# Dealing 1.5 MB of zeros to the DMA engines in other shares and from other SBUF rows, in a decode kernel that writes a gradient

## The chip, the cores and the metric

One core of one Trainium2 chip runs the whole program in one launch. The metric is the device time of that launch in microseconds, the median of several runs. One run was also recorded by the hardware profiler; its trace has every instruction, and every packet that the core's 16 DMA engines moved, with start, length, bytes and queue. A packet's record does not say which of the 16 engines moved it.

## The reference

A decode step of attention beside a gated feed-forward block, and the gradient of both. Four batch rows (`B = 4`), one token each, model width 512, 32 query heads on 8 key/value heads of width 128, a cache of 4096 positions of which only the last 1024 take part:

```python
k = jnp.repeat(k_cache[:, :, Sk - W:, :], rep, axis=1)     # W = 1024, Sk = 4096
v = jnp.repeat(v_cache[:, :, Sk - W:, :], rep, axis=1)
scores = jnp.einsum("bhqd,bhkd->bhqk", q, k) * (Dh ** -0.5)
p = _softmax(scores, axis=-1)
o = jnp.einsum("bhqk,bhkd->bhqd", p, v)
...
return x + _A_ref(xn, ...) + _B_ref(xn, ...)
...
_out, _vjp = jax.vjp(_f, A_x, A_k_cache, A_v_cache, A_wq, A_wo, B_w_gate, B_w_up, B_w_down)
_grads = _vjp(grad_out)
```

The gradients of the two caches have the shape of the whole caches. For the 3072 positions ahead of the window they are zero, and these zeros have to be written: 2 caches x 4 batches x 8 heads x 3072 x 128 numbers of 2 bytes, 50.3 MB. All of the data moved, weights, windows, gradients and zeros, is 111.9 MB.

## The kernel before

Five engines work side by side: TensorE multiplies, VectorE and ScalarE transpose, mask and empty the accumulators, GpSimd (POOL in the profile) clears tiles and copies small blocks, and SyncE (SP) issues nearly all transfers, in an order written out by hand. A transfer that SP issues goes through SP's own queue, a transfer that GpSimd issues through GpSimd's queue, and both are carried out by the same 16 DMA engines.

The stages in order: the weights of the feed-forward block and of the attention are loaded (lines 161 to 166 and 325 to 328); the feed-forward block and its gradients (up to line 451); the key and value windows, two buffers each, and per batch the scores, the softmax, and the gradients of keys and values (the loop at line 675); the last phase from line 769 on, in which the gradients of `wo` and `wq` are made in eight pieces of 1 MB and stored through `result` (line 116).

**The zeros.** `ztile` (line 223) holds zeros, 128 partitions of 12,288 bytes. The zeros to be written are cut into 32 groups of two heads (`ztodo`, line 281), 1.5 MB each. Such a group is 64 rows by 2 heads, 128 pieces of 12,288 bytes: row `m` is positions `48 m` to `48 m + 47`, and a piece is one row of one head. `zeros(n)` (line 298) lets SP write the next `n` groups: 64 rows are read from every second partition of `ztile`, each row for two pieces. `result` calls it ahead of each store by the counts in `before` (line 114); the loads of keys and values are followed by it too (lines 461 to 463, 731, 752). `zeros` makes a group wait for the group four earlier (`deep`).

31 of the 32 groups go that way. The last of the list, `zog, zb, zg` (line 283), is GpSimd's: `part_zeros(m0, rows, each, part, after)` (line 285) writes `rows * each` rows of it from `m0` on. Its source is `rows` partitions of `ztile`, starting at partition `part` and four apart, and each of them serves `2 * each` pieces. Before the change there are four calls: three on lines 422 to 424, right after GpSimd cleared its tiles of the feed-forward stage, while the weights are still loading (15 + 2 + 15 rows, from 3, 2 and 3 partitions), and one on line 819, at the start of the last phase (32 rows from 8 partitions), which waits for the group of SP last issued there (`zdone[-1]`).

So in the code before, the number of pieces for one source partition is 10, 2 and 10 in the three early calls, and 8 in the late one.

**Waits of SP.** Besides data and buffers, a transfer of SP waits until the completion semaphore that it is given is free. There are eight of them, given out in turn, so a transfer waits for the one eight before it.

Of the kernel before, what the change touches and what calls it, by code (L numbers as in the profile page):

```python
# [19 lines left out]
def kernel(  # L20
# [24 lines left out]
    nc = tc.nc  # L45
# [7 lines left out]
    K0 = Sk - W  # L53
# [29 lines left out]
    def evac(out, in_, n):  # L83

        ca, cd = (190 + n) / 1.2, (130 + n) / 0.96
        eng = "act" if load["act"] + ca <= load["dve"] + cd else "dve"
        load[eng] += ca if eng == "act" else cd
        if eng == "act":
            return nc.scalar.copy(out=out, in_=in_)  # L89
        return nc.vector.tensor_copy(out=out, in_=in_)  # L90

    def t32(out, in_, n):
        load["dve"] += (130 + n) / 0.96
        nc.vector.transpose(out=out, in_=in_)  # L94

    def pairs(ap):
        return ap.bitcast(U32)

    def scratch():
        return scrp.tile([P, 1024], U32, name="scr", tag="scr")  # L100
# [6 lines left out]
    def stg_tile():  # L107

        if not halves:
            pair = stg_pair()  # L110
            halves.extend(pair[:, h] for h in range(2))
        return halves.pop(0)
# [3 lines left out]
    def result(*parts):  # L116
        zeros(min(before.popleft(), len(ztodo)))
        for out, in_ in parts:
            nc.sync.dma_start(out=out, in_=in_)
# [19 lines left out]
    def mm(out, lhsT, rhs, first=True, last=True, pos=None):  # L139
        kw = {} if pos is None else {"tile_position": pos}  # L140
        nc.tensor.matmul(out, lhsT=lhsT, rhs=rhs, start=first, stop=last, **kw)  # L141

    def bank(name, tag="w", shape=(P, 512), dt=FP32):
        pool = {"w": ps_w, "x": ps_x}.get(tag, ps_a)
        return pool.tile(list(shape), dt, name=name, tag=tag)
# [75 lines left out]
    ZP = P // 2  # L221
    ZW = K0 // ZP * Dh
    ztile = const.tile([P, ZW], BF16, name="ztile")
# [36 lines left out]
    def window(dram, b, h):  # L260

        return dram[b, h * G // 2:(h + 1) * G // 2, K0:Sk, :].rearrange("g (m j) d -> m g (j d)", j=2 * J)

    def alternate(tl, h):

        t_ = tl[h:h + 1]
        return bass.AP(tensor=t_.tensor, offset=t_.offset,
                       ap=[[2 * t_.ap[0][0], P // 2], [2 * J * Dh, G // 2], [1, 2 * J * Dh]])

    def load_kv(b, k, pool, tag, eng, **kw):  # L270
        d_, src = ((k_t, A_k_cache), (v_t, A_v_cache))[k]
        tl = pool.tile([P, G // 2, 2 * J, Dh], BF16, name=tag, tag=tag)
        for h in range(2):
            with tc.high_priority():
                d = eng.dma_start(out=alternate(tl, h), in_=window(src, b, h), **kw)
        d_[b] = tl
        return d

    ZG = 2
    zsrc = bass.AP(tensor=ztile.tensor, offset=ztile.offset, ap=[[2 * ztile[:].ap[0][0], ZP], [0, ZG], [1, ZW]])  # L280
    ztodo = [(og, b, g) for b in range(B) for g in range(0, G, ZG) for og in (out_2, out_3)]
    zdone = []
    zog, zb, zg = ztodo.pop()

    def part_zeros(m0, rows, each, part, after=None):

        z = nc.gpsimd.dma_start(  # L287
            out=zog[zb, zg:zg + ZG, 0:K0, :].rearrange("g (m j) d -> m g (j d)", m=ZP)[m0:m0 + rows * each],
            in_=bass.AP(tensor=ztile.tensor, offset=ztile[part:part + 1, :].offset,
                        ap=[[4 * ztile[:].ap[0][0], rows], [0, ZG * each], [1, ZW]]))  # L290
        if after is not None:
            behind(z.ins, after.ins)

    def behind(ins, other):
        tc.add_manual_dep(ins, other.name,
                          mybir.DependencyInfo(mybir.DependencyClass.Sync, mybir.DependencyReason.DATA))

    def zeros(n, after=None, deep=4):

        for _ in range(n):  # L300
            og, b, g = ztodo.pop(0)
            z = nc.sync.dma_start(out=og[b, g:g + ZG, 0:K0, :].rearrange("g (m j) d -> m g (j d)", m=ZP), in_=zsrc)
            if len(zdone) >= deep:
                behind(z.ins, zdone[-deep].ins)
            if after is not None:
                behind(z.ins, after.ins)
            zdone.append(z)


    if True:  # L310
# [5 lines left out]
        def flat(t_):  # L316
            return t_[:].rearrange("p f c -> p (f c)")
# [92 lines left out]
        for wi, (wsb, dh, og) in enumerate(((wu_sb, dhu, out_7), (wg_sb, dhg, out_6))):  # L410
            dh_f = flat(dh)
            dhr = hgu[:].rearrange("p u f c -> p (u f c)").bitcast(BF16)
            for a, q in enumerate(quad):
                ps = bank("rep_ps", "w", (P, FQ))
                mm(ps[:], rsum_b[q, :], dh_f[q, :], pos=(Q * a, 0))
                evac(dhr[:, a * FQ:(a + 1) * FQ], ps[:], FQ)
            dhP = scratch()[:, 0:FPB * Q].rearrange("p (f x) -> p f x", f=FPB)
            t32(dhP, pairs(dhr[:, 0:F]), 896)
            dhs = ffn.tile([P, FPB, 2, 4 * B], BF16, name="dhs", tag=f"dhs{wi}")
            nc.gpsimd.memset(dhs[:], 0.0)  # L420
            if wi == 1:
                part_zeros(0, 3, 5, 0)
                part_zeros(15, 2, 1, 12)
                part_zeros(17, 3, 5, 20)
            dhPb = dhP.bitcast(BF16).rearrange("p f (x r) -> p f r x", r=2)
            for a, q in enumerate(quad):
                nc.vector.tensor_copy(out=dhs[q, :, :, a * B:(a + 1) * B], in_=dhPb[q, :, :, 0:B])
            for ch in range(4):
                sc = scratch()
                n7 = FPB // 4  # L430
                t32(sc[:, 0:n7 * P].rearrange("p (k c n) -> p c k n", k=n7, c=C),
                    pairs(wsb[:])[:, :, ch * n7 * Q:(ch + 1) * n7 * Q], 896)
                sb = sc[:, 0:n7 * P].bitcast(BF16).rearrange("p (k n r) -> p k r n", k=n7, r=2)
                for k in range(n7):
                    c = nm % 4
                    mm(dxf_ps[quad[c]].rearrange("p r n -> p (r n)"), dhs[:, ch * n7 + k].rearrange("p r x -> p (r x)"),
                       sb[:, k], nm < 4, nm >= 2 * FPB - 4, (0, Q * c))
                    nm += 1
            dwg_v = og.rearrange("(p h c) f -> h p (c f)", h=2, c=2)
            for h in range(2):  # L440
                stg = stg_tile()
                for ci in range(2):
                    for a, q in enumerate(quad):
                        ps = bank("dwg_ps", "w", (P, FQ))
                        mm(ps[:], xn_b[q, 2 * h + ci:D:C], dh_f[q, :], pos=(Q * a, 0))
                        o_ = (ci * NQ + a) * FQ
                        evac(stg[:, o_:o_ + FQ], ps[:], FQ)
                result((dwg_v[h], stg[:, 0:2 * F]))
# [4 lines left out]
    with tc.tile_pool(name="mid", bufs=1, reuse_waits="tile") as mid:  # L453
# [4 lines left out]
        with (tc.tile_pool(name="kvp", bufs=1, reuse_waits="tile") as kvp,  # L458
              tc.tile_pool(name="att", bufs=1, reuse_waits="tile") as att):
            load_kv(0, 1, kvp, "va", nc.sync)  # L460
            zeros(2)
            load_kv(1, 0, kvp, "kb", nc.sync)
            zeros(4)


# [2 lines left out]
            rows = [qm[:], dyBD[:].rearrange("p n r x -> p (n r x)").rearrange("p (b g d) -> p b g d", b=B, g=4)]  # L468
# [132 lines left out]
            def small(name, shape=(P, 1)):  # L601
                return att.tile(list(shape), FP32, name=name, tag=name)
# [72 lines left out]
            for b in range(B):  # L675
                S = sps[0][:]
                m = small("m")
# [124 lines left out]
            for i in range(KH):  # L802
                t, e, c = i // 8, i // 4 % 2, i % 4
# [12 lines left out]
            s_o = sums[:, 0:D]  # L816
            TT(out=s_o, in0=ob_ps[:], in1=fo[:], op=ALU.add)

            part_zeros(32, 8, 4, 64, zdone[-1])
            dwo_v = out_5.rearrange("(p t k) n -> t p (k n)", t=4, k=8)  # L820
            dwq_v = out_4.rearrange("(p c) j -> c p j", c=C)
            late = {}
# [126 lines left out]
```

## Time and profile before

| | |
|---|---|
| median of 3 runs | 272.11 us (272.02 to 273.19) |
| the profiled execution | 272.15 us |
| its span in the trace | 270.4 us |
| data moved | 111.90 MB, mean 414 GB/s; 30.68 MB read from and 81.01 MB written to HBM |
| busy share: PE, DVE, ACT, POOL | 61%, 67%, 51%, 13% |
| packets | 16,640 |

The span is the profiled execution between its first and last instruction; the 1.75 us between it and the 272.15 us lie around it. Times in the trace count from the start of the span. "SPq" and "POOLq" are an engine's issuing of transfers, not the transfer itself. A transfer of 1.5 MB of zeros takes SP about a microsecond to issue and lands about 19 us later.

### The profile page before, as it was taken

What the parts mean: (1) busy time and instruction counts of PE and PEld (TensorE: products, weight loads), DVE (VectorE), ACT (ScalarE), POOL (GpSimd) and SP (SyncE); (2) the same over time, 40 slices, a digit from 0 to 9 for tenths busy, and PEclk for the clock granted to TensorE, in tenths of its full rate; (3) what the DMA queues carried; (4) which work ended last, traced back from release to release, by engine and by line L of the source; (5) the groups of instructions that cost most, each with busy time, mean ns of one, the idle gap of its engine ahead of it and who ended that gap; (6) DMA issues with size and microseconds to landing.
All of it is one profiled execution on the core that took longest, in us unless ns stands there. A gap on an engine that the chain in (4) does not pass through costs nothing.

```text
span 270.4 us, 3304 instructions
## 1 busy us (share of the span) xinstructions
PE 164.6 (61%) x1152; PEld 62.0 (23%) x1159; DVE 180.5 (67%) x339; ACT 137.4 (51%) x278; POOL 36.1 (13%) x95
## 2 busy tenths in 40 slices
PE   1256988968536687676568578585877898460000
PEld 0121342222112342123222233122421223010000
DVE  7869768978798428873588536793289999970000
ACT  2242775670022636696577765696476666460000
POOL 8900002091032101120012100000000000000000
PEclk9998885556855555997999975997577999555555
DMA  7999999999999999999999999999999999999994
GB/s 264 437 422 449 409 369 425 430 431 413 421 426 428 430 412 425 426 421 427 415 421 418 433 416 421 431 422 431 418 428 425 422 429 417 429 429 428 428 420 207
DMA packets 16640, 111.90 MB, mean 414 GB/s; under 512 B 1760, under 2 KB 1776, under 8 KB 10992
## 3 DMA queue, kind: packets, MB, share of 16 engines
q1 hardware_dynamic: 16072, 110.12, 97.7%
q0 software_dynamic: 544, 1.57, 1.5%
q8 instruction: 9, 0.15, 0.2%
q14 instruction: 7, 0.06, 0.1%
q10 hardware_dynamic: 8, 0.00, 0.0%
HBM read 30.68 MB, written 81.01 MB: 413 GB/s over the span
## 4 chain that ended last, share of the span: by engine, by line
DVE 21%; PE 21%; ACT 17%; issue 4%; ACTq 0%
DVE scr L94 9%; ACT stg L124 6%; ACT spr L584 5%; PE kv_ps L141 4%; PE dw_ps L141 4%; DVE stg L124 3%; PE sc_ps L141 3%; PE ok_ps L141 2%; DVE odt L647 2%; PE od_ps L141 2%; ACT late L124 2%; DVE dqs L763 2%; DVE wq_t L94 2%; PE ob_ps L141 1%; ACT last L124 1%
## 5 line engine op out<-in xcount | busy, mean ns | idle before, releaser
L124 ACT CAST stg<-kv_ps 128x512 bf16<-128x512 f32 x102 | 54.6, 598 | 26.5 <-PE kv_ps L141 26.4
L141 PE MATMUL sc_ps<-scr,bd 128*32 128x256 bf16 x256 | 20.1, 399 | 18.1 <-DVE scr L94 17.5
L141 PEld LDWEIGHTS <-spr 128*128 128x128 bf16 x256 | 17.0, 108 | 36.1 <-issue 24.3
L141 PE MATMUL kv_ps<-dyBD,spr 128*128 128x512 bf16 x60 | 24.1, 528 | 1.9 <-issue 1.3
L141 PE MATMUL kv_ps<-qm,spr 128*128 128x512 bf16 x63 | 19.7, 387 | 3.0 <-DVE stg L124 1.1
L94 DVE STREAM_TRANSPOSE scr<-va 128x1024 uint32<-128x1024 uint32 x16 | 19.5, 1224 | 0.0
L124 DVE CAST stg<-kv_ps 128x512 bf16<-128x512 f32 x10 | 6.6, 688 | 17.9 <-PE kv_ps L141 17.9
L89 ACT CAST stg<-dwg_ps 128x448 bf16<-128x448 f32 x26 | 12.0, 567 | 3.3 <-DMA out_dram<-stg 2.4
L549 POOL COPY bd<-D3q 32x64 bf16<-32x64 bf16 x32 | 7.6, 245 | 44.4 <-PE sc_ps L141 43.2
L141 PEld LDWEIGHTS <-bd 128*32 128x32 bf16 x256 | 6.3, 99 | 29.8 <-issue 27.2
L141 PE MATMUL dw_ps<-scr,xn_b 32*128 32x512 bf16 x32 | 9.4, 545 | 5.5 <-ACT late L124 4.0
L124 ACT CAST late<-dw_ps 128x512 bf16<-128x512 f32 x16 | 9.2, 588 | 6.8 <-PE dw_ps L141 6.7
L141 PE MATMUL do_ps<-scr,dyBD 128*128 128x512 bf16 x31 | 11.1, 491 | 2.3 <-DVE scr L94 1.9
L584 ACT ACTIVATE spr<-dS_b,amask 64x256 bf16<-64x256 bf16 x16 | 7.4, 554 | 8.5 <-DVE dS_b L728 8.5
L549 POOL COPY bd<-D3d 32x64 bf16<-32x64 bf16 x32 | 7.4, 239 | 31.7 <-PE sc_ps L141 16.4
L647 DVE SCALAR_TENSOR_TENSOR odt<-od_ps,om,odt 128x128 f32<-128x128 f32 x12 | 4.2, 351 | 11.1 <-ACT odt L642 10.8
L124 DVE CAST stg<-dw_ps 128x512 bf16<-128x512 f32 x16 | 10.5, 685 | 1.5 <-PE dw_ps L141 1.3
L287 POOL DMA_DIRECT2D out_dram<-ztile x4 | 3.0, 753 | 61.9 <-DMA out_dram<-ztile 61.9
L94 DVE STREAM_TRANSPOSE scr<-wo_sb 128x1024 uint32<-128x1024 uint32 x8 | 9.8, 1237 | 1.6 <-PE do_ps L141 1.0
L124 ACT CAST stg<-dw_ps 128x512 bf16<-128x512 f32 x16 | 8.9, 588 | 3.6 <-PE dw_ps L141 3.4
L94 DVE STREAM_TRANSPOSE scr<-ka 128x1024 uint32<-128x1024 uint32 x8 | 9.8, 1233 | 1.2 <-PE r_ps L141 1.1
L124 DVE CAST late<-dw_ps 128x512 bf16<-128x512 f32 x16 | 10.4, 675 | 0.3 <-PE dw_ps L141 0.3
(203 smaller groups left out, 337.4 us busy)
## 6 DMA issues: line engine op xcount, KB each, us to landing
out_dram<-ztile SPq DMA_DIRECT2D x31, 1536.0 KB, 19.1
out_dram<-stg SPq DMA_DIRECT2D x18, 1024.0 KB, 14.7
va<-in_A_v_cache_dram SPq DMA_DIRECT2D x8, 1024.0 KB, 14.3
out_dram<-stg SPq DMA_DIRECT2D x6, 896.0 KB, 11.9
wq_sb<-in_A_wq_dram SPq DMA_DIRECT2D x1, 4096.0 KB, 27.9
wo_sb<-in_A_wo_dram SPq DMA_DIRECT2D x1, 4096.0 KB, 37.3
ka<-in_A_k_cache_dram SPq DMA_DIRECT2D x4, 1024.0 KB, 15.6
kb<-in_A_k_cache_dram SPq DMA_DIRECT2D x4, 1024.0 KB, 19.0
```

Of the source, the lines that this page charges most:

```text
L89: return nc.scalar.copy(out=out, in_=in_)
L94: nc.vector.transpose(out=out, in_=in_)
L124: return nc.scalar.copy(out=out, in_=in_) if eng == "act" else nc.vector.tensor_copy(out=out, in_=in_)
L141: nc.tensor.matmul(out, lhsT=lhsT, rhs=rhs, start=first, stop=last, **kw)
L287: z = nc.gpsimd.dma_start(out=zog[zb, zg:zg + ZG, 0:K0, :].rearrange("g (m j) d -> m g (j d)", m=ZP)[m0:m0 + rows * each], in_=bass.AP(ten ...
L549: nc.gpsimd.tensor_copy(out=t_[q, :, :, g2, :, o_:o_ + 4], in_=src[q, b, g2])
L584: nc.scalar.activation(out=out, in_=in_, func=ACT.Copy, scale=amask[q, a:a + 1])
L647: STT(out=t_[:], in0=ps[:, g, :], scalar=(om, oms)[k][:, g:g + 1], in1=t_[:], op0=ALU.mult, op1=ALU.add)
L763: nc.vector.tensor_copy(out=dqs[q, :, :, :, a * B + b], in_=d3v[q])
```

## The change

The address of GpSimd's group is set up once as `zpart`. `part_zeros` reads partitions eight apart instead of four apart. The early calls become two: 5 rows from 5 partitions (0, 8, 16, 24, 32; 2 pieces each) and 32 rows from 8 partitions (40, 48, ... 96; 8 pieces each). The late call becomes two of 12 rows from 3 partitions each (104, 112, 120, then 0, 8, 16; 8 pieces each). The 3 rows that are left, 17 to 19, 6 pieces or 73,728 bytes, are written by SP in a new transfer, `rest_zeros(17, 20)`, between its load of `kb` and the four groups of zeros behind it. That transfer cuts the three rows of each of the two heads into 8 packets of 4608 bytes; its destination has the shape 2 x 8 x 2304, its source is 16 partitions.

```diff
+    zpart = zog[zb, zg:zg + ZG, 0:K0, :].rearrange("g (m j) d -> g m (j d)", m=ZP)
+
     def part_zeros(m0, rows, each, part, after=None):
 
         z = nc.gpsimd.dma_start(
-            out=zog[zb, zg:zg + ZG, 0:K0, :].rearrange("g (m j) d -> m g (j d)", m=ZP)[m0:m0 + rows * each],
+            out=zpart[:, m0:m0 + rows * each].rearrange("g m e -> m g e"),
             in_=bass.AP(tensor=ztile.tensor, offset=ztile[part:part + 1, :].offset,
-                        ap=[[4 * ztile[:].ap[0][0], rows], [0, ZG * each], [1, ZW]]))
+                        ap=[[8 * ztile[:].ap[0][0], rows], [0, ZG * each], [1, ZW]]))
         if after is not None:
             behind(z.ins, after.ins)
+
+    def rest_zeros(m0, m1):
+
+        n = (m1 - m0) * ZW // 8
+        nc.sync.dma_start(out=zpart[:, m0:m1].rearrange("g m e -> g (m e)").rearrange("g (k e) -> g k e", k=8),
+                          in_=bass.AP(tensor=ztile.tensor, offset=ztile.offset, ap=[[8 * ztile[:].ap[0][0], 16], [1, n]]))
...
             if wi == 1:
-                part_zeros(0, 3, 5, 0)
-                part_zeros(15, 2, 1, 12)
-                part_zeros(17, 3, 5, 20)
+                part_zeros(12, 5, 1, 0)
+                part_zeros(20, 8, 4, 40)
...
             load_kv(1, 0, kvp, "kb", nc.sync)
+            rest_zeros(17, 20)
             zeros(4)
...
-            part_zeros(32, 8, 4, 64, zdone[-1])
+            part_zeros(52, 3, 4, 104, zdone[-1])
+            part_zeros(0, 3, 4, 0, zdone[-1])
```

The instructions of TensorE, VectorE and ScalarE are the same, in the same order. GpSimd issues four transfers as before, two early and two late instead of three and one. SP issues one transfer more.

## The prediction

> **What bounds the kernel now.** First the page's slices, then its queues, then the busy time by stretches, then the issues at the end.
>
> ```profile
> DMA  7999999999999999999999999999999999999994
> GB/s 264 437 422 449 409 369 425 430 431 413 421 426 428 430 412 425 426 421 427 415 421 418 433 416 421 431 422 431 418 428 425 422 429 417 429 429 428 428 420 207
> ...
> q1 hardware_dynamic: 16072, 110.12, 97.7%
> q0 software_dynamic: 544, 1.57, 1.5%
> q8 instruction: 9, 0.15, 0.2%
> q14 instruction: 7, 0.06, 0.1%
> ```
>
> The 16 DMA engines are full from the first slice to the last. q1 is SP's queue, q0 GpSimd's; q8 and q14 fetch the program itself.
>
> ```profile
> 180.00:240.00 60.00, 45.10 (x303) 15.05 (x303) 47.29 (x87) 38.60 (x77) 0.65 (x1) 0.77 1.01 425
> 240.00:265.00 25.00, 1.83 (x7) 0.33 (x5) 2.58 (x4) 2.35 (x4) 0.00 (x0) 0.50 1.01 427
> 265.00:270.40 5.40, 0.00 (x0) 0.00 (x0) 0.00 (x0) 0.00 (x0) 0.00 (x0) 0.50 0.36 152
> ```
>
> Columns: the stretch, its length, busy time of PE, PEld, DVE, ACT, POOL, granted clock, DMA share, GB/s. From 243 us on no engine computes, and the DMA engines still work at 427 GB/s up to 265 us; then the share falls to 0.36.
>
> ```profile
> 241.20 0.61 SPq L302 DMA_DIRECT2D out_dram<-ztile  x1
> 243.78 4.03 SPq L119 DMA_DIRECT2D out_dram<-late  x2
> 249.90 3.99 SPq L119 DMA_DIRECT2D out_dram<-stg  x2
> ```
>
> SP issues its last store before 253.9 us, and the data of it lands until 268.9 us: 15 us of work are queued when nothing is left to compute. So bytes bound the kernel, and neither GpSimd's time nor an earlier landing of weights can move the end. The bytes are the same after the change. What is left is how evenly the 16 engines end.
>
> **How the engines end.** The packet records name no engine. But a packet starts 3 ns ahead of the end of the one before it on its engine, and each engine has the same known order of SP's packet sizes; strung together by these two rules, the records from 33 us on fall into 16 chains without a gap. Their last packets end at (us of the span):
>
> ```
> GpSimd's pieces     chains, end of the last packet
> call of 32 rows, 8  268.88  266.90 266.65 266.61 266.59 266.56 266.55 266.48
> 2nd call of 15, 10  267.72  267.57  266.51
> 1st call of 15, 10  267.56  267.33  267.22
> call of 2 rows,  2  268.93  265.11
> mean of the 16      267.20
> ```
>
> The pieces of the last call lie on eight chains, those of the third call on three others. The small transfers of 4 rows have 4 packets of 1 KB, and these lie on four chains, 267.56, 267.33, 267.22 and 265.11. Of the five chains without a third or fourth call, 265.11 must be one with 2 pieces, as it ends 2 us ahead of its three mates. So GpSimd's queue deals engines in turn, 0 to 2, 3 and 4, 5 to 7, 8 to 15, and small transfers go to 0 to 3; engine 3 ends at 265.11 and engine 4 at 268.93.
>
> Two chains end 1.2 us behind all others. Engine 4 has just 2 pieces, but its packets of 12,288 bytes take 476 ns in the mean, those of the other 15 chains 460 to 462: 248 of them make 4 us. The other, at 268.88, is one of the eight with 8 pieces. It carries two of q8's nine fetches (0.94 us each), its mates one or none, and its 4 KB packets take 161.0 ns against some 159.7 (512 of them, 0.7 us). After 268.93 the program needs 1.4 us to close (270.36), and 1.75 us lie around the span: 272.15 us, against the median of 272.11.
>
> **The change part by part.** A piece of 12,288 bytes takes 460 ns and moves its chain on by 457.
>
> ```profile
> out_dram<-ztile POOLq DMA_DIRECT2D x1, 768.0 KB, 11.9
> out_dram<-ztile POOLq DMA_DIRECT2D x2, 360.0 KB, 25.1
> out_dram<-ztile POOLq DMA_DIRECT2D x1, 48.0 KB, 21.9
> ```
>
> Columns: how many issues, the size of one, us until it landed.
>
> GpSimd's calls of 5, 8, 3 and 3 partitions are dealt in the same way: engines 0 to 4 (2 pieces each), 5 to 12 (8), 13 to 15 (8), 0 to 2 (8). Together: 0 to 2 have 10 as before, 3 and 4 have 2 as before, 8 to 15 have 8 as before, 5 to 7 have 8 instead of 10. The six pieces that these three lose (0.91 us each) are those which SP writes. So engine 4 stays at 268.93, the other late chain at 268.88, engine 3 at 265.11, and 5 to 7 come to 266.8, 266.7 and 265.6, where it gains nothing.
>
> SP's new transfer: 16 packets of 4608 bytes. The trace has none of this size. The nearest are 4096 bytes (median 159 ns) and 7168 (272 ns); between them, nearer the first, I take 175. How many engines share it isn't shown either. The 4-row transfers run on 4 engines, and every transfer with 64 or 128 rows on 16, so the outermost count seems to decide; here it is 2 on the side of HBM and 16 on the side of SBUF. I take 2, the count that both sides can be cut into by their outermost rows, on the engines that the small transfers use first: engines 0 and 1 get 8 packets, 8 x 0.175 = 1.40 us. They come from among 267.22, 267.33 and 267.56, and so end at 268.6 to 268.96. Bounds of the price: 8 x 0.159 = 1.27 and 8 x 0.272 = 2.18 us, so 268.5 to 269.7. If all 16 share it, each gets one packet: 0.16 to 0.27 us on all, and engine 4 ends at 269.1.
>
> [...]
>
> Other source partitions: GpSimd's pieces took 460 ns from partitions four apart, as SP's did from its own rows, so I put the move at nothing. Bounds: one piece of the 128 took 794 ns; one to three such on the engine that ends last would be 0.3 to 1 us; below nothing it can't go, as 460 is what every undisturbed packet of this size takes.
>
> Early and late: 74 pieces instead of 64 ahead of the weights, at most 8 on an engine instead of 10, so the weights land up to 0.9 us sooner; 48 instead of 64 later. This moves work in time on engines that are never idle, and costs nothing as long as each has something queued. The cover is the 15 us at the end; at 67 us, where SP's new transfer is put, four groups of 1.5 MB follow, and a group lands 19 us after its issue. GpSimd issues two transfers (0.75 us each) at each place; nothing of weight is queued behind them.
>
> The new transfer waits for its semaphore, and the next ones each for one a place later. Behind it stand the four groups, then `va` of the next batch, which waits for VectorE until 93.2 us anyway, 10 us after the groups are issued. Among the eight in flight one is then small, which takes 1.5 MB, 3.7 us at 427 GB/s, from what is queued; 19 us are there. I put it at nothing.
>
> Sum: the last packet at 268.93 (engine 4) or 268.96 (engine 0 or 1) instead of 268.93: 0 to 0.03 us, and with three chains that may end last instead of two I take 0.05. The forecast is 272.2 us.
>
> **Rivals.** All 16 share SP's transfer: 268.93 + 0.17 = 269.10, 272.3 us. For it: the source has 16 rows; against: the outermost 2 of the destination.
>
> Slower: engines 0 and 1 become the last. They carry 13 pieces' worth then, more than any other. From 1.37 us on (268.93 - 267.56) the price of SP's packets sets the end: by the upper bound of 2.18 us it is 269.7, 272.9 us; where packets that fit no other in size and place are drawn out to 460 ns as a whole piece, it is 3.7 us, 271.2 at the end and 274.4 us in all. For it: one kind of packet is drawn out on engine 4 all through. Against: 4608 bytes are little more than 4096.
>
> Faster: engine 4's 4 us are the matter of its neighbours' odd source rows, or of this execution, and are gone. Then the chain at 268.88 still stands, and engines 0 and 1 at 268.7 or so: no more than 0.2 us. If the second fetch too falls elsewhere and SP's transfer is spread, the end comes to some 267.7, 270.9 us. Even an even deal would end at 267.20, 1.7 us sooner. Against: the 476 ns are there from 48 to 241 us, while GpSimd's pieces moved only to 41 us and from 218.7 to 224.4.
>
> Starved: the smaller queue at 67 us runs dry on the engine that is ahead. At most the 3.7 us, about half of it, 274.0 us. Against: no DMA share below 1.00 in that stretch.
>
> **How the numbers follow.** Forecast 0.58, spread 0.12, engines 0 and 1 last 0.19, faster 0.09, starved 0.02. A measurement of this kernel tells 0.5%, 1.36 us, from no change: 270.75 to 273.47. The forecast, the spread and most of both other cases stay within it: faster 0.05, same 0.82, slower 0.13. The range goes from 271.4, half of the faster case, to 273.1, where SP's packets are at their upper bound with a little for the runs before (272.02 to 273.19).
>
> **What would show it.** In the changed trace the DMA share should still be full until 265 us, the last packet land at 268.9 to 269.0, POOLq show issues of 120, 768 and 288 KB, and a new line of 72 KB from SP. Packets of 4608 bytes on two chains, eight each, would show the two engines; one on each of 16, the spread. I'd be wrong if another chain than engine 4's, the one with two fetches or engines 0 and 1 ended last, if a stretch had a share below 1.00, or if the 476 ns went or moved.

## The result and the profile after

| | before | after |
|---|---|---|
| median of 14 runs each (before: the first three among them) | 272.81 us (272.02 to 274.77) | 275.57 us (273.87 to 277.22) |
| the profiled execution | 272.15 us | 274.99 us |
| its span | 270.4 us | 273.2 us |
| last packet of SP's queue, us of the span | 268.93 | 271.95 |
| mean end of the 16 chains | 267.07 | 268.46 |

The ratio is 1.0101, 95% interval [1.0070, 1.0131]: the changed kernel is 1% slower. The forecast of 272.2 us and its range up to 273.1 us were wrong.

First the page of the changed kernel: its slices, then its queues.

```profile
DMA  7999999999999999999999999999999999999993
GB/s 270 437 399 440 428 389 422 433 422 420 419 420 428 428 412 423 419 422 425 411 423 416 434 412 423 431 419 432 414 435 419 431 375 405 432 425 425 423 412 132
...
q1 hardware_dynamic: 16090, 110.19, 97.1%
q0 software_dynamic: 480, 1.50, 1.5%
q8 instruction: 9, 0.15, 0.2%
q14 instruction: 7, 0.06, 0.0%
```

The DMA engines are as full as before, and SP's queue carries the 0.07 MB that GpSimd's has lost. Bytes still bound the kernel. But two slices, the 33rd and 34th (218.6 to 232.2 us), move 375 and 405 GB/s with engines that count as busy, where the kernel before had 429 and 417 in the slices of the same number. The issues show the change as it was made, with the time to landing in the last column:

```profile
out_dram<-ztile POOLq DMA_DIRECT2D x1, 768.0 KB, 18.8
out_dram<-ztile POOLq DMA_DIRECT2D x2, 288.0 KB, 15.8
out_dram<-ztile POOLq DMA_DIRECT2D x1, 120.0 KB, 7.1
out_dram<-ztile SPq DMA_DIRECT2D x1, 72.0 KB
```

The 768 KB are now the early call, and the two of 288 KB are the late ones. They land 15.8 us after their issue; 768 KB in one late call took 11.9 us before. Next the changed kernel by stretches (stretch, length, busy time of PE, PEld, DVE, ACT, POOL, granted clock, DMA share, GB/s):

```profile
215.00:220.00 5.00, 5.00 (x49) 1.06 (x42) 3.09 (x5) 2.67 (x5) 0.00 (x0) 0.50 1.03 424
220.00:225.00 5.00, 4.80 (x32) 1.44 (x30) 3.50 (x7) 2.26 (x5) 0.00 (x0) 0.50 1.02 375
225.00:230.00 5.00, 4.38 (x23) 1.70 (x23) 4.07 (x10) 3.22 (x7) 0.00 (x0) 0.84 1.00 388
...
240.00:265.00 25.00, 2.08 (x8) 0.33 (x5) 2.77 (x5) 2.36 (x5) 0.00 (x0) 0.50 1.01 424
265.00:273.20 8.20, 0.00 (x0) 0.00 (x0) 0.00 (x0) 0.00 (x0) 0.00 (x0) 0.50 0.41 171
```

And the kernel before in the middle ones, in the same columns:

```profile
220.00:225.00 5.00, 4.57 (x50) 1.55 (x50) 4.36 (x9) 3.41 (x6) 0.00 (x0) 1.00 0.99 414
225.00:230.00 5.00, 4.09 (x25) 1.62 (x24) 4.51 (x11) 3.47 (x7) 0.00 (x0) 0.98 1.05 428
```

From 220 to 230 us the changed kernel moves 3.82 MB where the kernel before moved 4.21: (375 + 388) x 5 against (414 + 428) x 5, in kB. The 0.4 MB are 0.94 us of all engines at 420 GB/s. With a DMA share of 1.02 and 1.00 over fewer bytes, packets must have lasted longer. It is just the time in which the two late calls run (218.7 to 228.5 us), and the packet records say which packets these are. GpSimd's 48 late pieces take 571 ns in the mean instead of 461, and 15 of them 600 ns or more, up to 1046; none of the 64 late ones did before. SP's own packets of the same 12,288 bytes suffer as well: 493 ns in the mean between 217 and 230 us instead of 463, 17 of them 600 ns or more. The extra time is 48 x 0.11 + 220 x 0.03 = 12 us on 16 engines.

It does not fall evenly. The chains, strung together as for the prediction, end at 271.95, 271.22, 270.72, 270.45, 270.05, 269.49, 269.20, 268.59 and 268.55 us, and seven between 267.36 and 265.41. So the mean end moves by 1.39 us, from 267.07 (the mean of the 16 ends in the prediction's list, which gives 267.20 for it), and the last by 3.0.

### The profile page after: what moved, and what is told of

Its sections match the earlier page's. It is cut to its first block, busy times and chain, and to the rows that moved or that the text cites. A ratio compares the mean times of both kernels' runs of the same rounds, so it can differ in the third digit from the quotient of the medians.

```text
span 273.2 us, 3304 instructions
## 1 busy us (share of the span) xinstructions
PE 165.1 (60%) x1152; PEld 60.7 (22%) x1159; DVE 180.9 (66%) x339; ACT 136.7 (50%) x278; POOL 36.0 (13%) x95
## 4 chain that ended last, share of the span: by engine, by line
DVE 21%; PE 18%; ACT 14%; DMA 5%; issue 4%; DVEq 0%; SPq 0%; ACTq 0%
DVE scr L94 7%; DMA out_dram<-stg 5%; ACT stg L124 5%; PE dw_ps L141 5%; ACT spr L592 4%; PE kv_ps L141 3%; PE sc_ps L141 2%; DVE stg L124 2%; DVE odt L655 2%; ACT late L124 2%; DVE dqs L771 2%; PE od_ps L141 2%; PE ok_ps L141 2%; DVE wq_t L94 2%; DVE wq_sb L94 2%
## 5 line engine op out<-in xcount | busy, mean ns | idle before, releaser
L141 PE MATMUL kv_ps<-dyBD,spr 128*128 128x512 bf16 x60 | 23.0, 501 | 1.9 <-issue 1.3
L89 ACT CAST stg<-dwg_ps 128x448 bf16<-128x448 f32 x26 | 11.9, 563 | 3.3 <-DMA out_dram<-stg 2.4
```

## The experiments

**The theory and its rivals.** Theory A: every DMA engine has SBUF partitions of its own, the ones at which the kernel before reads GpSimd's pieces for it: 0 to 8 for engines 0 to 2, 12 and 16 for 3 and 4, 20 to 28 for 5 to 7, 64 to 92 for 8 to 15. So engine `e` of 0 to 7 has partition 4e, and engine 8 + e has 64 + 4e; its late pieces from there took 461 ns in the mean. A piece that another engine reads from there makes the packets of both wait; for this the author assumed that the owner reads there for SP's transfers too. Since the records name neither engine nor partition, this is a theory, and the runs test what follows from it. After the change the late calls read 0, 8, 16 on engines 0, 1, 2 (those of 0, 2, 4) and 104, 112, 120 on engines 13, 14, 15, whose own are 84, 88, 92. The kernel before reads 96 to 124 for no engine of GpSimd's calls. The author gave 96 + 4e to engine 8 + e, so that 104, 112 and 120 are those of 10, 12 and 14; e8 below bears this out. The rivals: two late transfers instead of one; work moved from late to early; the new shares; SP's new transfer; the step of eight partitions as such.

One table for all runs. "Drawn out" counts late pieces of 600 ns or more. "Loss" is the time by which the packets of 4096, 8192 and 12,288 bytes that start between 215 and 240 us lasted longer than 159, 309 and 460 ns, the medians of SP's packets of these sizes in the kernel before, per engine. Ratios are to the kernel before on the same chip; the last four columns are of the profiled execution.

| run | ratio [95%] | last packet | late pieces, mean ns | drawn out | loss, us |
|---|---|---|---|---|---|
| before | | 268.93 | 461 | 0 of 64 | 0.14 |
| after | 1.0101 [1.0070, 1.0131] | 271.95 | 571 | 15 of 48 | 1.00 |
| e1_all_early | 1.0081 [1.0052, 1.0110] | 271.17 | none | | 0.11 |
| e2_places_8_apart | 1.0124 [1.0094, 1.0154] | 273.56 | 758 | 37 of 64 | 1.96 |
| e3_places_4_apart | 1.0014 [0.9992, 1.0037] | 269.95 | 460 | 0 of 48 | 0.14 |
| e4_late_in_two_halves | 1.0016 [0.9991, 1.0040] | 269.04 | 463 | 0 of 64 | 0.17 |
| e5_change_own_places | 1.0001 [0.9976, 1.0026] | 269.28 | 461 | 0 of 48 | 0.13 |
| e6_early_8_apart | 1.0039 [1.0017, 1.0061] | 270.18 | 469 | 0 of 64 | 0.30 |
| e7_late_from_0 | 1.0100 [1.0069, 1.0130] | 271.88 | 697 | 31 of 64 | 2.64 |
| e8_late_from_96 | 0.9981 [0.9962, 1.0001] | 268.71 | 462 | 0 of 64 | 0.15 |
| e9_shares_by_ends | 1.0159 [1.0127, 1.0191] | 273.64 | 597 | 26 of 70 | 1.40 |
| e10_eight_each | 1.0109 [1.0095, 1.0123] | 272.19 | 465 | 0 of 64 | 0.19 |
| e11_shares_no_tiny | 1.0063 [1.0042, 1.0084] | 272.03 | 468 | 0 of 70 | 0.34 |
| e12_tiny_not_counted | 1.0074 [1.0048, 1.0099] | 270.45 | 460 | 0 of 70 | 0.08 |

**No late call (e1).** The changed kernel, with its two late calls moved up among the weight loads and their sources kept.

```diff
                 part_zeros(20, 8, 4, 40)
+                part_zeros(52, 3, 4, 104)
+                part_zeros(0, 3, 4, 0)
...
-            part_zeros(52, 3, 4, 104, zdone[-1])
-            part_zeros(0, 3, 4, 0, zdone[-1])
```

> The changed kernel with its two late transfers of GpSimd (12 rows from 3 partitions each) moved up among the weight loads, behind the other two; nothing else. Theory 1 (the late pieces, given to some engines while their neighbours write SP's own zeros, make packets wait for one another: 12,288-byte packets of 700 to 1046 ns from 218 to 228 us): the drawn-out packets of that stretch are gone, their mean from 220 to 240 us falls from 491 ns to about 462, and the time comes back to that of the kernel before, ratio 0.995 to 1.002. Theory 2 (reading source partitions eight apart is what costs): the same here in the late stretch, as nothing is read there. Theory 3 (the uneven shares, 13 pieces' worth on engines 0 and 1, or SP's new transfer): it stays as slow as the changed kernel, ratio 1.008 to 1.013.

The loss of the late stretch is gone (0.11 us). So the late pieces cause it. The time is not: 1.0081. By the time alone this run would fit the rival of the shares and SP's transfer; e5 below rules that one out. With all 122 pieces among the weight loads, the loss by the same three packet sizes from 25 to 75 us is 0.74 us per engine instead of 0.20, and the last packet lands at 271.17. This run says where the late loss comes from, but it is no undoing of the change, since it adds a loss of its own early, whose cause it leaves open.

**The places alone, late (e2).** The kernel before, with its late call reading 64, 72, ... 120.

```diff
-    def part_zeros(m0, rows, each, part, after=None):
+    def part_zeros(m0, rows, each, part, after=None, apart=4):
...
-                        ap=[[4 * ztile[:].ap[0][0], rows], [0, ZG * each], [1, ZW]]))
+                        ap=[[apart * ztile[:].ap[0][0], rows], [0, ZG * each], [1, ZW]]))
...
-            part_zeros(32, 8, 4, 64, zdone[-1])
+            part_zeros(32, 8, 4, 64, zdone[-1], 8)
```

> The kernel before with one number changed: its late transfer (32 rows, 8 partitions) reads partitions 64, 72, ... 120 instead of 64, 68, ... 92. Theory 1 (uneven late pieces): all of engines 8 to 15 still get theirs together, so the time stays that of the kernel before, ratio 0.997 to 1.003, and the mean of the 12,288-byte packets from 220 to 240 us stays near 462 ns. Theory 2 (places): drawn-out packets as in the changed kernel, mean 480 ns or more, ratio 1.005 to 1.013. Theory 3 (shares): 1.000.

The stretches of this kernel, columns as before:

```profile
215.00:220.00 5.00, 4.31 (x54) 1.07 (x50) 4.23 (x7) 3.41 (x6) 0.00 (x0) 1.00 1.04 417
220.00:225.00 5.00, 4.58 (x46) 1.45 (x44) 4.40 (x9) 2.91 (x6) 0.00 (x0) 1.00 1.01 338
225.00:230.00 5.00, 3.73 (x20) 1.62 (x20) 4.79 (x11) 3.69 (x7) 0.00 (x0) 1.00 0.98 360
```

One number in one line, the step of the late call's sources, gives the whole loss and more: 1.0124, with no other share, no new transfer and no work moved in time. The throughput falls to 338 GB/s with a share of 1.01. By theory A, with 96 to 124 given as above, the sources 64, 72, ... 120 lie on just four engines' partitions (those of 8, 10, 12 and 14). Two of the call's engines read from each, and by the assumption the owner reads there for SP as well; only 64 is read by its owner. GpSimd's longest piece takes 1900 ns and SP's longest packet 1662, more than three times 460.

**The change with the late places four apart (e3), and with all places its readers' own (e5).** Each is the changed kernel with its shares and SP's new transfer, and other source partitions. In e5 the call of 8 rows is split in two, 3 rows for engines 5 to 7 and 5 rows for 8 to 12. First the edit of e3, then that of e5, both against the changed kernel (`apart` is the step, 8 unless given).

```diff
-            part_zeros(52, 3, 4, 104, zdone[-1])
-            part_zeros(0, 3, 4, 0, zdone[-1])
+            part_zeros(52, 3, 4, 84, zdone[-1], 4)
+            part_zeros(0, 3, 4, 0, zdone[-1], 4)
```

```diff
-                        ap=[[8 * ztile[:].ap[0][0], rows], [0, ZG * each], [1, ZW]]))
+                        ap=[[4 * ztile[:].ap[0][0], rows], [0, ZG * each], [1, ZW]]))
...
-                part_zeros(20, 8, 4, 40)
+                part_zeros(20, 3, 4, 20)
+                part_zeros(32, 5, 4, 64)
...
-            part_zeros(52, 3, 4, 104, zdone[-1])
+            part_zeros(52, 3, 4, 84, zdone[-1])
```

> The changed kernel with its two late transfers reading partitions 84, 88, 92 and 0, 4, 8, the places that the kernel before has for these engines, instead of 104, 112, 120 and 0, 8, 16. Theory 1: still drawn out, ratio 1.006 to 1.013. Theory 2: back at the kernel before, 0.997 to 1.003, late mean near 462 ns. Theory 3: 1.008 to 1.013 without drawn-out packets being the matter.

> The change's shares of pieces and SP's new transfer, but every engine from 0 to 15 reads at 0, 4, ... 28 and 64, 68, ... 92, early and late; the call for engines 5 to 12 becomes two (5 to 7, 8 to 12). Theory A (each DMA engine has partitions of its own, engine e below 8 those from 4e on and engine 8 + e those from 64 + 4e on, and a piece read from another engine's makes both wait): no packet of 700 ns or more, the last packet at 268.8 to 269.3 as the shares alone give it, ratio 0.997 to 1.002. Rival B (only the late transfers of the change cost, whatever the early ones read): the same time as with four-apart late places alone, 1.0014, within 0.002. Rival C (shares and SP's transfer cost too): 1.004 or more. [...]

With the late places put back the ratio is 1.0014, with all of them 1.0001 [0.9976, 1.0026]. The late stretch of e5:

```profile
215.00:220.00 5.00, 5.00 (x42) 0.96 (x40) 3.01 (x5) 2.34 (x4) 0.00 (x0) 0.50 1.03 433
220.00:225.00 5.00, 4.80 (x39) 1.43 (x38) 3.88 (x7) 2.83 (x5) 0.00 (x0) 0.50 0.99 409
225.00:230.00 5.00, 4.44 (x25) 1.76 (x23) 3.53 (x9) 3.19 (x6) 0.00 (x0) 0.83 1.05 428
```

409 and 428 GB/s again, at the granted clocks of the changed kernel (0.50 and 0.83), so the clock isn't what took the throughput. The new shares, SP's new transfer, two late calls instead of one and the move from late to early all stand in e5, and together cost nothing that can be measured; the interval leaves room for 0.26%.

**The places alone, early (e6).** The kernel before, with its three early calls read from 0 to 16, 24 and 32, and 40 to 56, eight apart (`apart` as in e2).

```diff
-                part_zeros(0, 3, 5, 0)
-                part_zeros(15, 2, 1, 12)
-                part_zeros(17, 3, 5, 20)
+                part_zeros(0, 3, 5, 0, apart=8)
+                part_zeros(15, 2, 1, 24, apart=8)
+                part_zeros(17, 3, 5, 40, apart=8)
```

> The kernel before with its three early calls reading at 0, 8, 16, then 24, 32, then 40, 48, 56, the places that the change has for these engines; the late call is untouched. Theory A: engines 1 to 7 read what belongs to others; but SP's packets of that time fill SBUF from HBM or store other tiles, so it costs less than the late call did: ratio 1.002 to 1.009. Rival B (early reads cost nothing): 0.998 to 1.002.

1.0039 [1.0017, 1.0061], but not by drawn-out pieces: the 64 early pieces take 466 ns in the mean and one lasts 600 ns or more, just as before (465, one). The loss from 25 to 75 us is 0.31 us against 0.20, while that from 100 to 215 us is 0.98 against 0.53, where no piece of GpSimd runs; in the other runs it lies anywhere from 0.48 to 1.43. Where the 0.4% arises is open. In e3 the early sources are still eight apart, and its ratio of 1.0014 shows no such cost.

**Two transfers instead of one (e4).** The kernel before, with its late call cut in two of 16 rows each, from the same partitions.

```diff
-            part_zeros(32, 8, 4, 64, zdone[-1])
+            part_zeros(32, 4, 4, 64, zdone[-1])
+            part_zeros(48, 4, 4, 80, zdone[-1])
```

> The kernel before with its late transfer cut into two of 16 rows, from partitions 64 to 76 and 80 to 92: the same pieces, places and engines, but engines 8 to 11 begin theirs ahead of 12 to 15. Theory 1: if it is the head start of some engines over their neighbours that matters, drawn-out packets appear and the ratio is 1.003 to 1.010; if the two halves start within a piece of each other, 1.000 to 1.003. Theory 2 and theory 3: 1.000, mean near 462 ns.

1.0016 [0.9991, 1.0040], no drawn-out piece, the last packet at 269.04. The number of late calls is not the matter.

**The step or the owner (e7, e8).** The kernel before with its late call still four apart, but from other eights: 0 to 28, which by theory A are those of engines 0 to 7 while engines 8 to 15 read them, and 96 to 124, each 32 above the partition that its reader has in the kernel before.

```diff
-            part_zeros(32, 8, 4, 64, zdone[-1])
+            part_zeros(32, 8, 4, 0, zdone[-1])
```

```diff
-            part_zeros(32, 8, 4, 64, zdone[-1])
+            part_zeros(32, 8, 4, 96, zdone[-1])
```

> The kernel before with one number changed: the late transfer of engines 8 to 15 reads partitions 0, 4, ... 28 instead of 64, 68, ... 92, four apart as before. Theory A: all of it belongs to engines 0 to 7, so pieces and SP's packets are drawn out to 700 ns and more, mean of the 12,288-byte packets from 220 to 240 us at 475 ns or more, ratio 1.006 to 1.02. Rival D (what costs is the step of eight, by which several pieces meet in one group of partitions): four apart is free, 0.998 to 1.002.

> The kernel before with one number changed: the late transfer of engines 8 to 15 reads partitions 96, 100, ... 124. If engines share out the 128 partitions eight in a row (engine e from 8e on), 96 to 103 are engine 12's and so on, and it is as slow as with 0 to 28, ratio 1.006 to 1.02. [...]

The late call's issue and the stretches, first of e7 (from 0), then of e8 (from 96):

```profile
out_dram<-ztile POOLq DMA_DIRECT2D x1, 768.0 KB, 13.7
...
215.00:220.00 5.00, 3.87 (x22) 0.74 (x20) 3.89 (x7) 3.51 (x7) 0.00 (x0) 1.00 1.03 409
220.00:225.00 5.00, 4.99 (x50) 1.07 (x48) 3.42 (x6) 2.61 (x5) 0.00 (x0) 0.63 1.00 290
225.00:230.00 5.00, 4.80 (x39) 1.54 (x32) 3.82 (x7) 2.57 (x5) 0.00 (x0) 0.50 0.98 353
```

```profile
out_dram<-ztile POOLq DMA_DIRECT2D x1, 768.0 KB, 12.0
...
215.00:220.00 5.00, 4.89 (x41) 0.97 (x40) 3.49 (x6) 2.31 (x5) 0.00 (x0) 0.51 1.03 431
220.00:225.00 5.00, 5.00 (x44) 1.07 (x42) 3.21 (x6) 2.43 (x5) 0.00 (x0) 0.50 1.00 416
225.00:230.00 5.00, 4.42 (x27) 1.89 (x25) 3.16 (x6) 2.44 (x5) 0.00 (x0) 0.62 1.04 424
```

The two kernels differ in one number. From 0, the throughput falls to 290 GB/s, half of the 64 pieces are drawn out, up to 1096 ns, and so are 45 of SP's packets of that size, up to 1080 ns. From 96 nothing is: 416 and 424 GB/s, 462 ns. The step is four in both, and four apart from 0 cost 236 ns a piece. So it is the place that counts, as theory A has it, and 96 to 124 are as good for engines 8 to 15 as 64 to 92 (462 and 461 ns). The step of eight does harm because it leaves the readers' places. By theory A all 16 engines are hit in e7, eight as readers and eight as the ones read from, and its chains end within 3.0 us, from 268.84 to 271.88. In e2 they end from 265.06 to 273.56. So e7 has more loss (2.64 us against 1.96) and yet the earlier end: what counts is the loss of the chain that ends last.

**Another deal (e10).** The kernel before, with its three early calls made one of 8 rows from 0 to 28: eight pieces on each of the 16 engines, all from their own partitions.

```diff
-                part_zeros(0, 3, 5, 0)
-                part_zeros(15, 2, 1, 12)
-                part_zeros(17, 3, 5, 20)
+                part_zeros(0, 8, 4, 0)
```

> The kernel before with equal shares at the engines' own places: one early call of 32 rows from partitions 0, 4, ... 28 for engines 0 to 7 instead of three calls, the late one untouched; 8 pieces for every engine. If engine 4 is slow by 4 us whatever it is given, its six pieces more bring it from 268.93 to 271.7, with nothing drawn out in 218 to 228 us, and the ratio is 1.007 to 1.011. If its lag came from the unequal shares, it goes, the last packet is at 268.9 (the engine with two fetches), and the ratio is 0.997 to 1.002.

No piece is drawn out, and the ratio is 1.0109: engine 4, which the prediction had 4 us behind by its own packets, now has eight pieces instead of two. Its last packet lands 272.19 - 268.93 = 3.26 us later, 0.54 us for each of the six. By 0.457 us a piece it is 2.74; the rest is open. The trace has a loss of 0.80 us per engine from 75 to 100 us (0.09 before), where no piece runs, but that it is this execution's alone is not shown, as all four runs lie between 275.07 and 275.62 us. One chain sets the end: the next one ends at 269.76. An even deal of pieces costs as much as the change did, by another way.

**Shares by the chains' ends (e9, e11, e12).** Could a version beat the kernel before? e9 was to give engines 3 and 4 no piece at all, by a transfer of 2 rows of 128 bytes that was only to take their turn; then 4 rows for engines 5 to 8 from 52 to 64, and late 7 rows for 9 to 15 from their own 68 to 92. That 52 to 60, 32 above 20 to 28, go with engines 5 to 7 was the author's assumption; no run shows it for 52 and 56, while engine 7's late pieces from 60 in e12, below, took 460 ns. SP writes the last two rows of each head (`rest_zeros`, two transfers of 4 packets). `CUT` is 64 numbers, the 128 bytes, and the definitions of `CUT`, `zpart` and `rest_zeros` are left out here.

```diff
+    def skip_two():
+
+        nc.gpsimd.dma_start(out=zpart[:, 62, 0:CUT],
+                            in_=bass.AP(tensor=ztile.tensor, offset=ztile[12:13, :].offset,
+                                        ap=[[4 * ztile[:].ap[0][0], 2], [1, CUT]]))
...
-                part_zeros(15, 2, 1, 12)
-                part_zeros(17, 3, 5, 20)
+                skip_two()
+                part_zeros(15, 4, 3, 52)
...
+            rest_zeros()
...
-            part_zeros(32, 8, 4, 64, zdone[-1])
+            part_zeros(27, 7, 5, 68, zdone[-1])
```

> All of GpSimd's pieces at the engines' own places, and other shares: engines 0 to 2 get 10, 3 and 4 only a packet of 128 bytes that moves the turn on, 5 to 8 get 6 (partitions 52, 56, 60, 64), 9 to 15 get 10 (late, partitions 68 to 92); the two rows left are written by SP in two transfers of 4 rows each, one piece's worth for each of engines 0 to 3. From the ends of the kernel before, 0.457 us a piece: engine 4 from 268.93 to 268.0, the engine with two program fetches from 268.88 to 268.0, engines 0 to 2 to at most 268.0, 9 to 15 to 267.4 to 267.8. If the last of the 16 ends sets the time and the two late chains are always the same, the last packet is at 267.8 to 268.3 and the ratio 0.995 to 0.999; if the late ones change with the shares or from run to run, 0.999 to 1.003.

It is the slowest of all, 1.0159, and the late pieces are drawn out, 26 of 70. So they don't come from their readers' own partitions, and one of the assumed turns is wrong. Two more runs moved the sources back by two engines (12 to 24 early, 60 to 84 late), e11 without the small transfer, e12 with it. The edit of e12 against e9, then that of e11 against e12 (where `CUT` is 0, so that SP also writes the 128 bytes):

```diff
-                part_zeros(15, 4, 3, 52)
+                part_zeros(15, 4, 3, 12)
...
-            part_zeros(27, 7, 5, 68, zdone[-1])
+            part_zeros(27, 7, 5, 60, zdone[-1])
```

```diff
-                skip_two()
```

> The shares of the experiment before the last without its transfer of 2 x 128 bytes: GpSimd's calls of 3, 4 and 7 rows, read from partitions 0 to 8, 12 to 24 and 60 to 84, four apart. If GpSimd's queue deals 3, 4 and 7 engines in turn (0 to 2, 3 to 6, 7 to 13), every piece comes from its engine's own partitions: late pieces 460 ns in the mean, none of 600 or more. Then engine 4 has 6 pieces instead of 2 and 4 us of its own lag, so about 4 x 0.457 = 1.8 us behind 268.9: the last packet at 270.0 to 270.8 us, 1.004 to 1.007. If calls of 7 rows are dealt otherwise, the late pieces are drawn out again (mean over 550 ns, 15 or more of 600 and above) and the last packet lands after 272 us.

> The same sources as in the run beside it, but with the transfer of 2 x 128 bytes ahead of the call of 4 rows. If that small transfer does not move GpSimd's turn, the late pieces take 460 ns with none of 600 or more, and the time is that of the run beside it within 0.3%. If it moves the turn by 2, the late call runs on engines 9 to 15 while its sources belong to engines 7 to 13: late pieces above 550 ns, 15 or more of 600 and above, the last packet later by 2 us or more than in the run beside it, 1.01 or more. If it moves the turn by another count, the late pieces are drawn out too, and this run alone can't tell which.

The late stretch of e9, then of e12:

```profile
220.00:225.00 5.00, 5.00 (x46) 1.06 (x42) 3.04 (x5) 2.34 (x4) 0.00 (x0) 0.50 1.00 370
225.00:230.00 5.00, 4.81 (x30) 1.81 (x29) 3.29 (x7) 2.32 (x5) 0.00 (x0) 0.50 1.02 368
```

```profile
220.00:225.00 5.00, 4.80 (x32) 1.46 (x32) 3.55 (x7) 2.31 (x5) 0.00 (x0) 0.50 1.01 422
225.00:230.00 5.00, 4.45 (x24) 1.66 (x23) 4.09 (x10) 3.25 (x7) 0.00 (x0) 0.84 1.02 419
```

With the sources of e12 the pieces take 460 ns and none is drawn out, with the small transfer and without it. So that transfer did not move the turn, and in e9 engines 7 to 13 had read what belongs to 9 to 15. e12 is also the control for the changed kernel's fall: PE's busy time and the granted clocks are the same in both stretches (4.80 and 4.38 or 4.45; 0.50 and 0.84), and the throughput is 422 and 419 GB/s, not 375 and 388. e11 and e12 stay 0.6 and 0.7% behind the kernel before, which fits the six pieces that engine 4 now has. Four more by 0.457 us make 1.8; e12's last packet is 1.5 us later than before. The time of e11 is as expected, but its last packet, at 272.03, missed its expectation of 270.0 to 270.8; its profiled execution is the longest of its five, and it lost 1.43 us per engine from 100 to 215 us (0.53 before), where no piece runs.

No version is clearly faster than the kernel before; e8, at 0.9981 [0.9962, 1.0001], can't be told from it.

## Why the prediction was wrong

**The step that failed** is the one on the source partitions: "GpSimd's pieces took 460 ns from partitions four apart, as SP's did from its own rows, so I put the move at nothing", with one to three pieces of 794 ns, 0.3 to 1 us, as its upper bound. The move is the whole effect as far as can be measured: the last packet is 3.0 us later with it (after) and 0.35 us later without it (e5). Four things were missing in that step:

- The 460 ns of the kernel before were of pieces that were all their readers' own, so the row was no price for other places. The deal of engines that the prediction had worked out (0 to 2, 3 and 4, 5 to 7, 8 to 15) stood against sources 0 to 28 and 64 to 92, and this is a pattern: engine `e` reads partition `4e`, engine `8 + e` reads `64 + 4e`. The prediction took it for a step of four.
- The price was sought on GpSimd's pieces alone. SP's packets of the same stretch lasted longer too, 493 ns in the mean instead of 463: 220 x 0.03 = 6.6 us of some 12 in all.
- The 794 ns piece was the wrong row. One early piece of 600 ns or more is also there in e5, where every place is its reader's own.
- "Below nothing it can't go" was right, but the upper end held a few pieces; 15 of 48 late ones were drawn out, with 17 packets of SP.

The runs agree with this pattern. Late sources laid by it, or 32 above it (all of e8, one in e11 and e12), ran at 460 to 469 ns in the mean (before, e3 to e6, e8, e10 to e12); calls with sources beside it ran at 571 to 758 (after, e2, e7, e9). Set against the deal of engines, it shows the step's weak place: of the late sources 104, 112, 120, 0, 8 and 16, only 0 is the partition that its reader had in the kernel before. The pattern gives no price.

**From the loss to the end.** The packets' extra time over the whole run grew from 1.09 to 2.43 us per engine, 0.86 of it between 215 and 240 us. The growth of 1.35 us is about the 1.39 by which the mean end moved. The other 1.6 us of the 3.0 are unevenness, which the prediction had rightly called what is left when bytes bind. (By the right mean of 267.07, its even deal would end 1.9 us sooner than the kernel before, not 1.7.) The chain that ends last, at 271.95, carries drawn-out late pieces and also three of SP's packets of 600 ns or more. The chains that end at 271.22, 270.72 and 270.45 carry no late piece at all, and the first two carry seven and six such packets of SP. This fits what theory A has of engine 14, which reads another's partitions while its own are read, and of engines that are read from but have no late piece; 4, 10 and 12 would be these. As the records name no engine, it is not shown for each.

One thing does not fit the simple form of theory A. The second late call's pieces lie on three chains, and on two of them they take 460 ns in the mean, though by the theory only engine 0 reads its own partitions. So one misplaced source cost nothing there. Why is open.

**What held.**

- Bytes bind: the share in the changed kernel's stretches stays at 1.00 or more until 265 us, and no engine computes from 243 us on.
- GpSimd's queue deals engines in turn across calls of 5, 8, 3, 3, and so in e5 of 5, 3, 5, 3, 3: the late sources that e3 and e5 lay by it run at 460 and 461 ns, none of 48 drawn out.
- SP's new transfer takes two engines: 16 packets of 4608 bytes, 178 ns each, on two chains of eight, from 83.4 to 85.2 us. SP's queue has 1342 packets of 4 bytes, 83 x 16 + 3 x 4 + 2 if a transfer leaves one on each engine that it takes; before the change it had 1340. The price is 8 x 0.178 = 1.42 us (predicted: 1.40).
- The shares, the move in time and the wait of the new transfer cost nothing that can be measured: e5's last packet lands at 269.28, against 268.93 to 268.96 in the sum, and its ratio is 1.0001.
- Engine 4's lag belongs neither to one execution nor to one chip. An engine has 194 of SP's packets of 12,288 bytes between 48 and 215 us. The traces before, after and of e1, e2, e3, e5, e10 and e12 each have 139 to 178 such packets of 465 to 500 ns, 476 or 477 in the mean, and these six experiments ran on four chips. In e5, where all sources are their readers' own, they are there too.

**The rivals.** The time came out beyond both prices of the slower rival (272.9 and 274.4 us), and not by its mechanism: SP's packets of the new transfer took 178 ns, not 272 or 460. Of the signs that were to prove the forecast wrong, one came: other chains ended last. The 476 ns did not go (151 such packets between 48 and 215 us, 159 before). The share below 1.00 did not come, and could not have shown this cost, as a drawn-out packet counts as busy (1.02 at 375 GB/s). GB/s beside the share was the sign to name.

## What to carry to other kernels

When GpSimd issues a transfer from a few partitions, work out which DMA engines its rows are dealt to, and give each engine the partitions from which its pieces ran undisturbed: here late pieces took 460 to 469 ns from 4e, 64 + 4e and 32 above these, and 571 to 758 in calls with other places. The start counts as much as the step (e7, from 0: 697 ns; e8, from 96: 462). Look at GB/s beside the DMA share: full engines with fewer bytes (1.02 at 375 GB/s) were drawn-out packets here, and the packets of the other queue paid as well (493 ns instead of 463). Where bytes bind a kernel, count what the latest engine gets, for the mean end moved by 1.4 us here and the last by 3.0.

## What the runs showed of the hardware

- Late pieces read from partitions that by theory A are another engine's could take longer, and SP's packets of that time with them. In e7 GpSimd's late pieces took 697 ns in the mean instead of 461 and up to 1096, and SP's packets up to 1080; in e9 one piece took 1401. In e2, where by the theory two of the call's engines meet the owner's own reading, one piece took 1900 ns and one packet of SP 1662. Not every misplaced source did so (one in the changed kernel ran at 460). The price in e7 is some 240 ns in the mean for a piece of 460. Partitions 96 to 124 were as good for engines 8 to 15 (e8, 462 ns) as 64 to 92 (461). Why they are is open.
- The same misplacement cost GpSimd's pieces nothing among the weight loads: the changed kernel's 74 early pieces took 460 ns in the mean and none 600 ns. They ran from 15.4 to 29.6 us, while SP's queue loads `wq` and `wo` into SBUF; late, its stores and zeros read from it. That reads lengthen only reads is the author's guess, and was not tried by itself.
- A transfer of GpSimd of two rows of 128 bytes did not move the turn by which its queue deals engines (late pieces of 597 ns in e9, 460 in e12), while one of two rows of 12,288 bytes did (before: its 4 pieces lie on two chains, those of the next call on three others). Sizes between were not tried.
- One engine is 4 us slower than the other 15 over the whole run (476 ns for a packet of 12,288 bytes against 460 to 462), and traces of four chips show as many packets of that length as one engine would carry. Why is open.
